# RWKV attention and a relu-squared MLP on one core: w loaded as one row and spread by TensorE, PSUM banks given out by the planner, and the input matmul of units 8 to 19 for two units at a time

## The chip, the core and the metric

The kernel runs on one core of a Trainium2 chip. The metric is the device time of one execution in microseconds (us), as a median of runs. TensorE (PE) multiplies matrices and writes to PSUM; VectorE (DVE), ScalarE (ACT) and GpSimd (POOL) work elementwise; SyncE (SP) only issues transfers here. Each engine runs its own instructions in order and waits on semaphores for the others. Transfers are carried by 16 DMA engines, whichever queue issued them.

## The reference

A linear attention with decay over a sequence of 768, for 4 batches and 8 heads of 48, and behind it an MLP on the 3072 rows of 384 that it gives.

```python
for t in range(S):                                   # S = 768
    cur = einsum('bhd,bhe->bhde', u[None] * kt, vt)
    y[:, :, t] = einsum('bhd,bhde->bhe', rt, state + cur)
    state = w[None, :, :, None] * state + einsum('bhd,bhe->bhde', kt, vt)
x = y.transpose(0, 2, 1, 3).reshape(B * S, H * D)    # 3072 x 384
h = x @ w_in                                         # 384 x 2048
r = maximum(h, 0.0)
out = (r * r) @ w_out                                # 2048 x 384
```

## The kernel before

The sequence is cut into 6 chunks of 128 rows; a chunk of one batch is a unit, so there are 24 units, in the order chunk 0 of batches 0 to 3, chunk 1 of batches 0 to 3, and so on. Per unit:

- Three loads of r, k and v on SP's queue (L219, 192 KB each, in pieces of 192 bytes). VectorE scales r by powers of w and k by negative powers into `rkw` (L242, `wpos` and `wneg`), ScalarE casts v to `vb` (L246).
- `rkw` is turned into `rkT`: for the first NPE = 8 units by eight TensorE transposes into PSUM and one ScalarE copy (L262, L266), for the others by one DMA transpose on SP's queue (L251).
- `at`: eight matmuls of turned k by turned r (L279) into two PSUM banks; VectorE masks them into `am` (L287). `diag` (L293) and `dv` (L301) make the term with u. `s` (L309) and L321/L323/L327/L333 carry the state of the batch from chunk to chunk: add, decay, cast to `stb`. `y` (L341, and L347 with the state), then `yb` (L356).
- `yb` is turned into `xT`: for the first NPY = 6 units on TensorE with a ScalarE copy (L368, L372), for the others by a DMA transpose (L361).
- MLP, in four quarters of 512 hidden columns: the input matmul `m1` (L382, 12 matmuls of 128 columns into one bank `h`), relu on ScalarE (L390), square into `g` on VectorE (L398) for quarters 0 and 2 and on ScalarE (L396) for 1 and 3, and the output matmul `m2` (L405, 4 matmuls of 384 columns). Then the copy `osb` (L412) and the store (L416).

The weights are eight transfers on POOL's queue: four quarters of w_in (I0 to I3, L229) and four of w_out (O0 to O3, L233). In front of each stands a small POOL copy (L225) that reads k of some unit, so that a quarter is not issued before that load has landed. The list `front` in the planner's set-up gives the order of unit loads U and quarters: U0, U1, I0, U2, I1, U3, O0, I2, I3, U4, O1, O2, O3, U5. Each quarter is gated on the unit last named before it.

The set-up: w goes out to all partitions as one 192 KB broadcast (L153), and w and u also as columns by partition in four small scattered loads (L164), all on ScalarE's queue. ScalarE takes the logarithm (L176) and two powers (L178, L180). POOL makes `uwb` from the columns (L199, L202) and `wend`, the decay over a chunk, by a chain of squarings (L204, L206).

The order on each engine comes from a planner (`Plan`): each step has an engine, a cost, a rank, the steps it needs, and the buffers it opens and uses; the planner plays the program through with these costs and a lag after each step, and an engine takes the first step by rank whose needs are done and whose buffers are free. What it finds is issued in that order. PSUM is split into fixed pools: two banks for `at` and `s`, one for `y`, three for `h` (and for the turns), two for `o`.

Of the kernel before, what the change touches and what calls it, by code (L numbers as in the profile page):

```python
# [15 lines left out]
class Plan:  # L16
# [4 lines left out]

    def __init__(self):
        self.steps = []
        self.at = {}
        self.users = {}

# [8 lines left out]
    def run(self, room):  # L35
# [7 lines left out]
        queues = {e: [] for e in todo}  # L43
        order = []
# [7 lines left out]
        def fits(s):  # L52
            names = [x[0] for x in s["new"]]
            for name in set(names):
                ring, m = rings[name], room[name]
                for n in range(len(ring) - m, len(ring) - m + names.count(name)):
                    if n >= 0 and not all(done(x) for x in self.users[ring[n]]):
                        return False
            return True

        while left:
            for e, mine in todo.items():
                if free[e] > t + tiny:
                    continue
                for s in mine:
                    if s["move"] and sum(x[1] for x in queues[e]) > 4.0:
                        continue
                    if all(done(self.at[k]) for k in s["needs"]) and fits(s):
                        mine.remove(s)
                        left -= 1  # L70
                        for x in s["new"]:
                            rings[x[0]].append(x)
# [30 lines left out]
def kernel(  # L103
# [21 lines left out]
    NPE = 8  # L125
    NPY = 6
    NPAD = 4
    SQACT = (1, 3)
# [4 lines left out]
    xpool = ctx.enter_context(tc.tile_pool(name="xpool", bufs=6))  # L133
    gpool = ctx.enter_context(tc.tile_pool(name="gpool", bufs=8))
    mpool = ctx.enter_context(tc.tile_pool(name="mpool", bufs=6))
    ps_at = ctx.enter_context(tc.tile_pool(name="ps_at", bufs=2, space=PSUM))
    ps_y = ctx.enter_context(tc.tile_pool(name="ps_y", bufs=1, space=PSUM))
    ps_h = ctx.enter_context(tc.tile_pool(name="ps_h", bufs=3, space=PSUM))
    ps_o = ctx.enter_context(tc.tile_pool(name="ps_o", bufs=2, space=PSUM))
# [8 lines left out]
    tiles = [{} for _ in units]  # L148

    w_bc = const.tile([128, dm], F32)
    nc.scalar.dma_start(  # L153
        out=w_bc, in_=w.rearrange("h d -> (h d)").unsqueeze(0).to_broadcast([128, dm])
    )
    wcol = const.tile([128, HP], F32)
    ucol = const.tile([128, HP], F32)
    nc.vector.memset(wcol, 1.0)
    nc.vector.memset(ucol, 0.0)
    nc.scalar.preload_act_table_set("natural_log_exp_and_others")  # L160
    with nc.allow_non_contiguous_dma(reason="384 decay values by partition"):
        for x, src in ((wcol, w), (ucol, u)):
            for o in range(2):
                nc.scalar.dma_start(  # L164
                    out=x[o * 64 : o * 64 + D, :],
                    in_=src.rearrange("(p o) d -> o d p", o=2)[o],
                )
# [7 lines left out]
    lnw = const.tile([128, dm], F32)  # L175
    nc.scalar.activation(lnw, w_bc, AF.Ln)  # L176
    wpos = const.tile([128, H, D], F32)
    nc.scalar.activation(wpos.rearrange("p h d -> p (h d)"), lnw, AF.Exp, scale=up)  # L178
    wneg = const.tile([128, H, D], F32)
    nc.scalar.activation(wneg.rearrange("p h d -> p (h d)"), lnw, AF.Exp, scale=down)  # L180
# [18 lines left out]
    nc.gpsimd.tensor_tensor(ucol, ucol, wcol, ALU.mult)  # L199
    for o in range(2):  # L200
        sl = slice(o * 64, o * 64 + 64)
        nc.gpsimd.tensor_copy(uwb.rearrange("p a h -> p (a h)")[sl, o :: H + 2], ucol[sl, :])  # L202
    wend_c = const.tile([128, HP], F32)
    nc.gpsimd.tensor_tensor(wend_c, wcol, wcol, ALU.mult)  # L204
    for _ in range(6):
        nc.gpsimd.tensor_tensor(wend_c, wend_c, wend_c, ALU.mult)  # L206
# [6 lines left out]


# [41 lines left out]
    def turn(i, x):  # L256
        t = tiles[i]
        if x == 0:
            t["tp"] = ps_h.tile([128, 2, HP, C], BF16, name="h")
            t["rkT"] = work.tile([128, 2, HP, C], BF16, name="rkT")  # L260
        for p in range(HP):
            nc.tensor.transpose(t["tp"][:, x, p, :], t["rkw"][:, x, p].rearrange("p o e -> p (o e)"), identb)  # L262

    def evict_rk(i):
        t = tiles[i]
        nc.scalar.copy(t["rkT"], t["tp"])  # L266
# [6 lines left out]
    def at(i):  # L273
        t = tiles[i]
        t["at"] = [ps_at.tile([C, HP, C], F32, name="at") for o in range(2)]
# [7 lines left out]

    def mask(i, o):
# [4 lines left out]
    def diag(i):  # L289
        t = tiles[i]  # L290
        t["y"] = ps_y.tile([C, dm + H], F32, name="y")
# [13 lines left out]
    def state_mm(i):  # L305
        t = tiles[i]
        t["s"] = ps_at.tile([128, HP, 2 * D], F32, name="at")
# [49 lines left out]

    def x_dma(i):
        t = tiles[i]
        t["xT"] = xpool.tile([128, NK, C], BF16, name="xT")  # L360
        nc.sync.dma_start_transpose(out=t["xT"], in_=t["yb"])  # L361

    def x_turn(i):
        t = tiles[i]
        t["tp"] = ps_h.tile([128, NK, C], BF16, name="h")
        t["xT"] = xpool.tile([128, NK, C], BF16, name="xT")
# [7 lines left out]
    def mm1(i, q):  # L374
        t = tiles[i]
        if q == 0:
            t["g"] = gpool.tile([128, NF, C], BF16, name="g")
        t["h", q] = ps_h.tile([128, 4, C], F32, name="h")
        for a in range(4):
            f = q * 4 + a  # L380
            for n in range(NK):
                nc.tensor.matmul(  # L382
                    out=t["h", q][:, a, :], lhsT=w_in_sb[:, n, f * 128 : (f + 1) * 128],
                    rhs=t["xT"][:, n, :], start=(n == 0), stop=(n == NK - 1),
                )

    def relu(i, q):
        t = tiles[i]
        t["gr", q] = mpool.tile([128, 4, C], F32, name="gr")
        nc.scalar.activation(t["gr", q], t["h", q], AF.Relu)  # L390

    def square(i, q):
        t = tiles[i]
        g = t["g"][:, q * 4 : q * 4 + 4, :]
        if q in SQACT:
            nc.scalar.activation(g, t["gr", q], AF.Square)  # L396
        else:
            nc.vector.tensor_tensor(g, t["gr", q], t["gr", q], ALU.mult)  # L398

    def mm2(i, q):  # L400
        t = tiles[i]
        if q == 0:
            t["o"] = ps_o.tile([128, dm], F32, name="o")
        for f in range(q * 4, q * 4 + 4):
            nc.tensor.matmul(  # L405
                out=t["o"], lhsT=t["g"][:, f, :], rhs=w_out_sb[:, f, :],
# [6 lines left out]

    def store(i):
# [5 lines left out]
    plan = Plan()  # L420
    PE, ACT, DVE, POOL, SP = "PE", "ACT", "DVE", "POOL", "SP"
    L1, L2 = 10, 16
# [4 lines left out]
    def add(*a, lag=0.30, **kw):  # L427
        plan.add(*a, lag=lag, **kw)

    def copy(*a, **kw):  # L430
        plan.add(*a, lag=1.20, **kw)

    add("w", ACT, 6.0, None, rank=-1e3)
    copy("begin", SP, 0.74, None, rank=-1e3, move=(0.6, 16))
    front = ['U0', 'U1', 'I0', 'U2', 'I1', 'U3', 'O0', 'I2', 'I3', 'U4', 'O1', 'O2', 'O3', 'U5']
# [11 lines left out]
    for i in range(NU):  # L447
# [3 lines left out]
        rank = place.get(f"U{i}", a - 20)  # L451
# [5 lines left out]
        for x in range(2):  # L457
            add(
                ("scale", i, x), DVE, 0.48, do(scale, i, x), rank=a - 4 + 0.1 * x,
                needs=[("rt", i) if x == 0 else ("kt", i), "w", ("scale", i - 1, x) if i else None],  # L460
# [3 lines left out]
            ("vb", i), ACT, 0.44, do(cast_v, i), rank=a + 0.5, needs=[("vt", i), ("scale", i, 1)],  # L464
# [3 lines left out]
        if i < NPE:  # L468
            add(("turn", i, 0), PE, 0.25, do(turn, i, 0), rank=a, needs=both[:1], new=[("h", i, "rk"), ("rkT", i)], uses=[("rkw", i)])
            add(  # L470
                ("turn", i, 1), PE, 0.25, do(turn, i, 1), rank=a - 0.1, needs=[both[1], ("turn", i, 0)],
                uses=[("h", i, "rk"), ("rkw", i)],
            )
            add(("rkT", i), ACT, 0.95, do(evict_rk, i), rank=a, needs=[("turn", i, 1)], uses=[("h", i, "rk"), ("rkT", i)])
        else:
            copy(("rkT", i), SP, 0.45, do(turn_dma, i), rank=a - 30, needs=both, move=(2.0, 32), new=[("rkT", i)], uses=[("rkw", i)])
        add(("rk", i), DVE, 0.37, do(rk, i), rank=a + 1, needs=[("rkT", i)], new=[("rk", i)], uses=[("rkT", i)])
        add(
            ("at", i), PE, 0.43, do(at, i), rank=a + 1, needs=[("rkT", i)], new=[("at", i, 0), ("at", i, 1)], uses=[("rkT", i)],
        )  # L480
        for o in range(2):
            add(
                ("mask", i, o), DVE, 0.645, do(mask, i, o), rank=a + 1 + 0.1 * o, needs=[("at", i)],
                new=[("am", i, o)], uses=[("at", i, o)],
            )
        add(("diag", i), PE, 0.11, do(diag, i), rank=a + 2, needs=[("rk", i)], new=[("y", i)], uses=[("rk", i)])
        add(("dv", i), DVE, 0.5, do(diag_v, i), rank=a + 2, needs=[("diag", i), ("vb", i)], new=[("dv", i)], uses=[("y", i), ("vb", i)])
        if c < NCH - 1:
            add(
                ("s", i), PE, 0.17, do(state_mm, i), rank=a + 2.1, needs=[("scale", i, 1), ("vb", i), ("at", i)],  # L490
# [3 lines left out]
                ("sadd", i), DVE, 0.6, do(state_add, i), rank=a + 2.2,  # L494
                needs=[("s", i), ("stb", before) if c else None], uses=[("at", i, 2)],
            )
            if c > 0:
                add(("sdec", i), DVE, 0.27, do(state_decay, i), rank=a + 4 + 2, needs=[("sadd", i)])
            add(
                ("stb", i), ACT, 0.6, do(state_cast, i), rank=a + 6 + 2,  # L500
                needs=[("sdec" if c else "sadd", i), ("y", before) if c else None],
            )
        add(
            ("y", i), PE, 0.38 if c else 0.21, do(y_mm, i), rank=a + 3,
# [3 lines left out]
        add(("yb", i), DVE, 0.5, do(evict_y, i), rank=a + 3, needs=[("y", i), ("dv", i)], new=[("yb", i)], uses=[("y", i), ("dv", i)])  # L508
# [62 lines left out]
```

## Time and profile before

| | |
|---|---|
| median of three runs | 181.29 us (181.0 to 181.76) |
| the profiled run | 181.37 us |
| its span, first to last instruction | 179.6 us |
| outside the span | 1.77 us |
| last output matmul ends | 176.24 us |
| first turn of `rkw` on TensorE | 6.19 us |
| first input matmul | 17.16 us |
| DMA: all bytes, mean rate | 28.53 MB, 159 GB/s |
| the unit loads, stores and transposes (queue 1) | 74.5% of 16 engines' span |
| the weights (queue 0) | 10.9% |
| the set-up loads (queue 10) | 0.8% |

The page has a row of busy tenths for each engine in 40 slices of 4.49 us. The chain of waits follows the work that ended last back to the start. In a timeline each line has a start, a length, the engine, the line of the kernel, the operation, output and inputs, and in brackets how long the engine stood idle before it and what released it. Lengths of matmul groups there include the modelled end of the last matmul; the chain has only the time until the next group begins. Issues of DMA transfers that each engine makes are shown with a q behind the engine's name.

The weights' quarters, from their issue to their landing in the profiled run: I0 11.01 to 17.1, I1 13.65 to 20.4, O0 18.69 to 24.1, I2 19.58 to 27.4, I3 20.44 to 29.8, O1 23.13 to 32.5, O2 24.02 to 35.2, O3 24.88 to 37.9. The loads of k: unit 0 lands at 6.7, unit 1 at 10.0, unit 2 at 13.1, unit 3 at 18.1, unit 4 at 22.5, unit 5 at 38.5.

### The profile page before, as it was taken

To read this page: it belongs to the slowest core of one execution; us is meant where nothing else is said; L and a number is where in the kernel's file an instruction comes from. 1 tells how busy PE (TensorE), PEld (TensorE's weight loads), DVE (VectorE), ACT (ScalarE), POOL (GpSimd) and SP (SyncE) were. 2 spreads that over 40 slices of the span, in tenths; PEclk is the share of its full clock that TensorE was granted. 3 is DMA by queue.
4 is the path that set the end of the run, shared out by engine and by line. 5 is a ranking of instruction groups with operands and counts; after the bars stand their busy time and mean duration, and the time that the engine had idled before them with its cause. 6 is when DMAs were issued, how large, how long until landed. Compare 5 with 4: busy or idle time off the path is not lost.

```text
span 179.6 us, 5414 instructions
## 1 busy us (share of the span) xinstructions
PE 164.1 (91%) x2258; PEld 130.3 (73%) x2258; DVE 135.6 (76%) x288; ACT 130.1 (72%) x250; POOL 11.2 (6%) x36
## 2 busy tenths in 40 slices
PE   0257798999999999999999999999999999999992
PEld 0135696887787877788878778787877877787861
DVE  3268859875899999999899699789969957763310
ACT  3636378988889788497787878866885876659751
POOL 2261650000000000000000000000000000000000
PEclk9999999999999999999999999999999999999999
DMA  4999999999998998979799878799869799122002
GB/s 95 184 180 207 212 194 185 185 182 179 188 194 184 154 192 163 192 159 173 171 178 201 157 160 159 138 194 218 162 116 216 144 139 273 59 66 69 17 29 89
DMA packets 107432, 28.53 MB, mean 159 GB/s; under 512 B 100624, under 2 KB 107408, under 8 KB 107408
## 3 DMA queue, kind: packets, MB, share of 16 engines
q1 hardware_dynamic: 102720, 24.85, 74.5%
q0 software_dynamic: 3712, 3.15, 10.9%
q10 hardware_dynamic: 976, 0.20, 0.8%
q8 instruction: 17, 0.28, 0.7%
q14 instruction: 7, 0.06, 0.1%
HBM read 20.65 MB, written 4.72 MB: 141 GB/s over the span
## 4 chain that ended last, share of the span: by engine, by line
PE 86%; DMA 9%; SPq 1%; DVE 1%; issue 0%; ACT 0%; POOL 0%; POOLq 0%
PE h L382 37%; PE o L405 35%; DMA kt<-in_k_dram 6%; PE at L279 4%; DMA w_in_sb<-in_moe_w_in_dram 4%; PE y L341 2%; PE y L347 2%; PE at L309 2%; PE h L262 2%; PE y L293 1%; SPq L219 1%; DVE rkw L242 1%; PE h L368 0%; DVE yb L356 0%; ACT osb L412 0%
## 5 line engine op out<-in xcount | busy, mean ns | idle before, releaser
L382 PE MATMUL h<-xT,w_in_sb 128*128 128x128 bf16 x1152 | 81.6, 223 | 1.3 <-DMA w_in_sb<-in_moe_w_in_dram 1.3
L382 PEld LDWEIGHTS <-w_in_sb 128*128 128x128 bf16 x1152 | 71.9, 100 | 9.4 <-DMA w_in_sb<-in_moe_w_in_dram 1.7
L390 ACT ACTIVATE gr<-h 128x512 f32<-128x512 f32 x96 | 56.8, 596 | 27.0 <-PE h L382 26.3
L405 PE MATMUL o<-w_out_sb,g 128*128 128x384 bf16 x384 | 75.9, 326 | 0.0
L405 PEld LDWEIGHTS <-g 128*128 128x128 bf16 x384 | 33.2, 98 | 14.9
L398 DVE TENSOR_TENSOR g<-gr 128x512 bf16<-128x512 f32 x48 | 32.9, 688 | 12.0 <-ACT gr L390 11.7
L287 DVE TENSOR_TENSOR am<-at,smask 128x512 bf16<-128x512 f32 x48 | 30.9, 684 | 9.6 <-PE at L279 9.5
L396 ACT ACTIVATE g<-gr 128x512 bf16<-128x512 f32 x48 | 30.1, 630 | 1.1
L242 DVE TENSOR_TENSOR rkw<-rt,wpos 128x384 bf16<-128x384 f32 x24 | 13.2, 552 | 4.6 <-ACT wpos L178 2.9
L333 ACT CAST stb<-st 64x192 bf16<-64x192 f32 x40 | 13.9, 347 | 3.1 <-DVE st L321 2.6
L262 PE MATMUL h<-identb,rkw 128*128 128x128 bf16 x64 | 7.8, 264 | 9.0 <-DVE rkw L242 8.8
L412 ACT COPY osb<-o 128x384 f32<-128x384 f32 x24 | 11.5, 479 | 6.2 <-PE o L405 5.8
L246 ACT CAST vb<-vt 128x384 bf16<-128x384 f32 x24 | 12.2, 507 | 3.7 <-DMA vt<-in_v_dram 3.5
L356 DVE TENSOR_TENSOR yb<-y,dv 128x384 bf16<-128x384 f32 x24 | 13.4, 557 | 2.0 <-PE y L347 0.7
L242 DVE TENSOR_TENSOR rkw<-kt,wneg 128x384 bf16<-128x384 f32 x24 | 13.2, 551 | 1.4 <-DMA kt<-in_k_dram 1.4
L301 DVE TENSOR_TENSOR dv<-vb,y 128x384 f32<-128x384 bf16 x24 | 13.1, 545 | 1.4 <-PE y L293 1.4
L323 DVE TENSOR_TENSOR st<-at,st 64x192 f32<-64x192 f32 x32 | 11.3, 354 | 1.8 <-PE at L309 1.6
L262 PEld LDWEIGHTS <-rkw 128*128 128x128 bf16 x64 | 4.9, 115 | 10.7 <-DVE rkw L242 10.3
L271 DVE TENSOR_TENSOR rk<-rkT 128x512 bf16<-128x512 bf16 x24 | 10.0, 418 | 1.9 <-ACT rkT L266 1.9
L279 PE MATMUL at<-rkT 64*128 64x128 bf16 x192 | 10.4, 229 | 0.0
L341 PE MATMUL y<-vb,am 128*128 128x48 bf16 x192 | 8.9, 186 | 0.9 <-DVE dv L301 0.9
L279 PEld LDWEIGHTS <-rkT 64*128 64x128 bf16 x192 | 5.9, 98 | 4.4 <-issue 2.3
(40 smaller groups left out, 82.1 us busy)
## 6 DMA issues: line engine op xcount, KB each, us to landing
rt<-in_r_dram SPq DMA_DIRECT2D x24, 192.0 KB, 4.5
kt<-in_k_dram SPq DMA_DIRECT2D x24, 192.0 KB, 4.4
vt<-in_v_dram SPq DMA_DIRECT2D x24, 192.0 KB, 4.5
out_dram<-osb SPq DMA_DIRECT2D x24, 192.0 KB, 2.7
w_in_sb<-in_moe_w_in_dram POOLq DMA_DIRECT2D x4, 384.0 KB, 7.3
w_out_sb<-in_moe_w_out_dram POOLq DMA_DIRECT2D x4, 384.0 KB, 10.3
xT<-yb SPq DMA_TRANSPOSE x18, 3.2
rkT<-rkw SPq DMA_TRANSPOSE x16, 3.2
```

What stands on the lines that cost most here:

```text
L242: nc.vector.tensor_tensor(t["rkw"][:, x, :, :, :D], pair(src), pair(wx), ALU.mult)
L262: nc.tensor.transpose(t["tp"][:, x, p, :], t["rkw"][:, x, p].rearrange("p o e -> p (o e)"), identb)
L279: nc.tensor.matmul(out=t["at"][o][:, p, :], lhsT=t["rkT"][sl, 1, p, :], rhs=t["rkT"][sl, 0, p, :], start=True, stop=True,)
L287: nc.vector.tensor_tensor(am, t["at"][o], smask.unsqueeze(1).to_broadcast([C, HP, C]), ALU.mult)
L301: nc.vector.tensor_tensor(t["dv"], t["vb"], t["y"][:, dm:].unsqueeze(2).to_broadcast([C, H, D]), ALU.mult)
L333: nc.scalar.copy(stb[b][sl, :, o * D : (o + 1) * D], st32[b][sl])
L356: nc.vector.tensor_tensor(t["yb"], t["y"][:, :dm], t["dv"].rearrange("p h d -> p (h d)"), ALU.add)
L382: nc.tensor.matmul(out=t["h", q][:, a, :], lhsT=w_in_sb[:, n, f * 128 : (f + 1) * 128], rhs=t["xT"][:, n, :], start=(n == 0), stop=(n == N ...
L390: nc.scalar.activation(t["gr", q], t["h", q], AF.Relu)
L396: nc.scalar.activation(g, t["gr", q], AF.Square)
L398: nc.vector.tensor_tensor(g, t["gr", q], t["gr", q], ALU.mult)
L405: nc.tensor.matmul(out=t["o"], lhsT=t["g"][:, f, :], rhs=w_out_sb[:, f, :], start=(f == 0), stop=(f == NF - 1),)
```

## The change

- w is loaded as one row (1.5 KB); its logarithm is taken on one partition and spread to all 128 by one fp32 matmul with a row of ones into a PSUM bank, from which both powers are taken. The columns of w and u are loaded as rows of four partitions on SP's queue behind unit 0's k, turned by two TensorE transposes, and copied by VectorE; POOL works from that copy, behind the issue of I0.
- One tile for each of the eight PSUM banks. The planner now gives a step the bank that has been free longest, with at most 4 for `at`, 2 for `y`, 5 for `h`, 2 for `o`.
- `xT` and `g` become tiles of a whole chunk (four units). The input matmul runs for the units in GROUPS: one at a time for units 0 to 7 and 20 to 23, and two at a time for units 8 to 19, in eight steps of six matmuls of 256 columns. Squares go to ScalarE (A) or VectorE (M) by a pattern over the steps, 5 of 8 on ScalarE.
- NPE is 7, NPY 10, NPAD 6. The ScalarE copy of `rkT` is made in two halves, one behind each four turns.
- The last unit's output matmul, copy and store are made in two halves of 192 columns, the second copy on VectorE.
- `front` is U0, I0, U1, U2, I1, U3, I2, U4, I3, O0, O1, O2, O3, U5. Ranks of loads, state steps and output matmuls, costs and the lag (0.15 for 0.30) are changed.

```diff
-    def run(self, room):
+    def run(self, room, banks, count):
...
+            wanted = [name for name in names if name in banks]
+            if wanted:
+                for n, x in held.items():
+                    if x is not None and all(done(u) for u in self.users[x]):
+                        held[n], since[n] = None, max(u["ready"] for u in self.users[x])
+                if sum(x is None for x in held.values()) < len(wanted):
+                    return False
...
-    NPE = 8
-    NPY = 6
-    NPAD = 4
-    SQACT = (1, 3)
+    NPE = 7
+    NPY = 10
+    NPAD = 6
+    SQUARES = 'AMAMAAAM'
+    GROUPS = (1,) * 8 + (2,) * 6 + (1,) * 4
...
-    nc.scalar.dma_start(
-        out=w_bc, in_=w.rearrange("h d -> (h d)").unsqueeze(0).to_broadcast([128, dm])
-    )
+    nc.scalar.dma_start(out=wrow, in_=w.rearrange("h d -> (h d)").unsqueeze(0))
...
+    def columns():
+        nc.sync.dma_start(out=wu[:, 0, :, :D], in_=w.rearrange("(p o) d -> p o d", o=2))
+        nc.sync.dma_start(out=wu[:, 1, :, :D], in_=u.rearrange("(p o) d -> p o d", o=2))
+
+    def spread_log():
+        spread["log"] = bank("h", "log")[:, :dm]
+        nc.tensor.matmul(out=spread["log"], lhsT=ones, rhs=lnw, start=True, stop=True)
+
+    def power(out, scale):
+        nc.scalar.activation(out.rearrange("p h d -> p (h d)"), spread["log"], AF.Exp, scale=scale)
+
+    def spread_columns():
+        spread["cols"] = bank("h", "cols")[:, : 2 * HP].rearrange("p (x a) -> p x a", x=2)
+        for x in range(2):
+            nc.tensor.transpose(spread["cols"][:, x, :], wu[:, x].rearrange("p o d -> p (o d)"), ident4)
...
-    def evict_rk(i):
+    def evict_rk(i, x=slice(None)):
         t = tiles[i]
-        nc.scalar.copy(t["rkT"], t["tp"])
+        nc.scalar.copy(t["rkT"][:, x], t["tp"][:, x])
...
+    def mm1(i, m, s):
...
+        for a in range(4 // m):
+            f = s * (4 // m) + a
+            for n in range(NK):
+                turned = w_in_sb[:, n, f * 128 : (f + 1) * 128]
+                nc.tensor.matmul(
+                    out=t["h", s][:, a], lhsT=turned, rhs=chunks[c]["xT"][:, n, b : b + m, :],
+                    start=(n == 0), stop=(n == NK - 1),
+                )
...
-    L1, L2 = 10, 16
+    L1, L2 = 10, 18
...
-    def add(*a, lag=0.30, **kw):
+    def add(*a, lag=0.15, **kw):
...
-    front = ['U0', 'U1', 'I0', 'U2', 'I1', 'U3', 'O0', 'I2', 'I3', 'U4', 'O1', 'O2', 'O3', 'U5']
+    front = ['U0', 'I0', 'U1', 'U2', 'I1', 'U3', 'I2', 'U4', 'I3', 'O0', 'O1', 'O2', 'O3', 'U5']
...
-        rank = place.get(f"U{i}", a - 20)
+        rank = place.get(f"U{i}", a - 24)
...
-        ld=6, rkw=NPAD, at=2, y=1, h=3, o=2, g=8, rkT=4, vb=4, rk=4, am=8, dv=4, yb=4, xT=6, gr=6, osb=6,
+        ld=6, rkw=NPAD, g=2, rkT=4, vb=4, rk=4, am=8, dv=4, yb=4, xT=3, gr=8, osb=8,
     )
-    for s in plan.run(room):
+    for s in plan.run(room, dict(at=4, y=2, h=5, o=2), len(banks)):
```

## The prediction

> **What bounds the kernel now.** I read the busy shares and the 40 slices first, then the chain of waits in the middle of the run, then the timeline of the first 30 us, because only there and at the very end TensorE is not full.
>
> ```profile
> PE 164.1 (91%) x2258; PEld 130.3 (73%) x2258; DVE 135.6 (76%) x288; ACT 130.1 (72%) x250; POOL 11.2 (6%) x36
> PE   0257798999999999999999999999999999999992
> DMA  4999999999998998979799878799869799122002
> ```
> ```profile
> 100.20 0.33 PE at L279 x8
> 101.28 0.08 PE y L293 x4
> 102.06 0.17 PE at L309 x4
> 102.23 0.65 PE o L405 x4
> 102.88 0.20 PE y L341 x8
> 103.07 0.17 PE y L347 x4
> 103.25 0.67 PE h L382 x12
> ```
> ```profile
> 8.74 2.21 POOL L206 TENSOR_TENSOR wend_c<-wend_c 128x4 f32<-128x4 f32 x6
> 11.01 0.92 POOL L229 DMA_DIRECT2D w_in_sb<-in_moe_w_in_dram  x1
> 13.65 0.78 POOL L229 DMA_DIRECT2D w_in_sb<-in_moe_w_in_dram  x1 [0.28 <-issue]
> ```
> ```profile
> 20.47 1.46 PE L382 MATMUL h<-xT,w_in_sb 128*128 128x128 bf16 x12 [0.63 <-DMA w_in_sb<-in_moe_w_in_dram]
> ...
> 23.23 1.49 PE L382 MATMUL h<-xT,w_in_sb 128*128 128x128 bf16 x12
> ...
> 28.96 0.83 PE L382 MATMUL h<-xT,w_in_sb 128*128 128x128 bf16 x12
> ...
> 45.15 0.40 PE L279 MATMUL at<-rkT 64*128 64x128 bf16 x8
> ```
>
> In the second fence (the chain at 100 us; start, length, step) every length is the time until TensorE issues its next step: input matmul of a quarter 0.67 (I use 0.668), output matmul of a quarter 0.65 (0.652), `at` 0.33, `diag` 0.10, `s` 0.17, `y` 0.20 plus 0.17 with a state. From the timeline at 40 us, four turns of `rkw` cost 0.22 and an x turn 0.17. Times the counts, that is 64.1 + 62.6 + 8.0 + 2.4 + 3.4 + 8.2 + 3.5 (16 half turns) + 1.0 = 153.2 us of TensorE work. TensorE ends its last output matmul at 176.24, so it loses 23.0 us in all. Adding the same prices along its order up to any step, and taking that from the step's start, gives the loss up to there: `at` of unit 5 starts at 45.15 with 24.2 us of work before it, loss 20.95. After that only 2.05 us are lost in 131, spread evenly, which prices rounded down explain. So the middle is bound by TensorE alone, and what an edit can win lies before 45 us or behind 176.24.
>
> The head loses its time in three ways. The weights come late (third fence): quarter 0 of w_in (I0) is issued at 11.01, after unit 1's k and a POOL chain of 2.21 us, and lands 6.1 us later; I1 lands at 20.47. The DMA row is full from slice 2 on. And twelve matmuls take 1.49 at 23.23 but 0.83 at 28.96: half speed until about 26.4 (a step at 26.48 is the first quick one), though the clock column shows 1.00 there. TensorE is dense from 20.47, so the speed came 5.9 us after that.
>
> **The change part by part.** *w as one row.* Gone: the 192 KB broadcast and four scattered column loads of ScalarE's queue. New: one row, a row of logarithms, one fp32 matmul, two powers read from PSUM. The row lands between 1.8 us after its issue at 0.73 (the last stores) and 3.6 (the broadcast): 2.5 to 4.3, I take 3.4. Ln is 0.52, the powers 0.61 each. The fp32 matmul is in no row; between one 384-column matmul (0.33) and four at half speed (1.3), I take 1.2, nearer the upper since it is cold and fp32. `wpos` then stands at 3.4 + 0.5 + 1.2 + 0.2 + 0.6 = 5.9 (5.54 before), `wneg` at 6.5. Unit 0's k lands at about 6.3 (6.69 before, less the broadcast's share), so this part is worth about 0, bounds -0.8 to +0.5. The two small loads in SP's queue behind k are 16 rows; two transposes on TensorE and a copy on VectorE stand in front of unit 0's second scale, which ends near 7.5 (7.33 before). The POOL chain, now behind I0's issue, ends near 10.3; its reader, the first state add, comes after the masks at about 11.3, so it is covered by 1 us.
>
> *The order of weights.* I0 is now gated on unit 0's k, I1 on unit 2's, I2 on unit 3's, I3 and all of w_out on unit 4's; the POOL chain moves behind I0. Loads that meet no weights land 1.0 apart (unit 2's r at 12.0, k at 13.07). A weight quarter occupies the DMA engines 2.45 (10.9% of the span, by 8). So: I0 issued 6.5, lands 12.6. Unit 2's k: 6.3 + 6 x 1.0 + 2.45 = 14.8; I1 issued 15.0, lands 6.1 to 6.8 later (both rows): 21.4. Unit 3's k 17.8, I2 lands about 24.8. Unit 4's k: 17.8 + 3 + 2 x 2.45 = 25.7; I3 lands 32.3. The four quarters of w_out are issued 0.85 apart and land 2.7 apart, as the last four did before (29.8, 32.5, 35.2, 37.9): 35.0, 37.7, 40.4, 43.1. So I0 comes 4.5 us sooner and the last quarter 5.2 us later.
>
> *What TensorE makes of it.* Unit 0 no longer waits for unit 1's turns: `at` starts near 8.9 (11.15 before), masks, `yb` and x turn follow as before and its first input matmul starts near 14.0 (17.16). From there TensorE is dense, so I expect full speed 5.9 later, at 20. In the new order the work before the first use of I1, I3, and each w_out quarter is 6.2, 15.5, 18.0, 20.6, 23.4 and 25.4. Losses at those gates: 21.4 - 6.2 = 15.2; 32.3 - 15.5 = 16.8; 17.0; 17.1; 17.0; 43.1 - 25.4 = 17.7. The last decides: 17.7 against 20.95, a gain of 3.25. Bounds: gates 2 us earlier or later (unit 4's k between no delay by I2 and waiting for all of it), so 1.25 to 5.25.
>
> *Half copies of the turned tile.* The copy of rkT is split in two halves of 0.5 (1.01 before). The second four turns write the bank that the first half is read from, and in the built program they carry a wait on ScalarE. Where they follow at once (units 2, 3 and 5) TensorE stands 0.4 to 0.7 each, 1.6 in all. I cost it at nothing, since the weights' gates end later; without that cover it is 1.6. The Trainium skill, PSUM — Partial Sum Buffer, Terms, says that TensorE and another engine may not touch one bank at the same time; this speaks against halving a copy in one bank, no row here shows such a collision, and by it the 1.6 could not be planned away.
>
> *Two units at a time.* 48 steps of six 256-column matmuls stand for 48 of twelve. A line through 128 columns (55.7 ns) and 384 (163 ns) gives 109.3, so 0.656 a step: 48 x 0.012 = 0.6 gained, bounds 0 to 0.8. The Trainium skill, TensorE: Matmul & The Clock Gate, Back-to-back issue gap, states 81 ns sustained at 128 columns and 131 at 512; an estimate between them, 98 at 256, would make it 48 x 0.38 = 18 us. The row, 0.67 for twelve, decides: weight loads are already hidden.
>
> *Counts.* Groups of four turns are 14 for 16 and x turns 10 for 6: -0.4 + 0.7 = +0.2. SP's queue so loses four x transposes and gains one of rkT; ScalarE gains four x copies of 0.475 and loses one of 1.01. With the pairs TensorE's work is 152.8, 0.4 less. Banks handed out by the planner, 5 of 8 squares on ScalarE: ScalarE gains about 12 x 0.63 = 7.6 us, VectorE loses 8; hidden behind TensorE, whose middle has no wait to remove. The pairs bunch input matmuls seven in a row, so I put 0.5 on the middle (0 to 9, priced below).
>
> *End.* From 176.24 to 179.6 is 3.36: a copy of 0.48, a store that lands 1.9 after issue, and the close. A copy of 192 columns is 0.35 (the state rows) and the store half as long: 3.0 (2.85 to 3.3).
>
> Sum: 176.24 - 3.25 - 0.4 + 0.5 + 3.0 = 176.1 span. The profiled run took 181.37, 1.77 more than its span: 177.9. The median of runs is 0.08 lower: **177.8**.
>
> **The rivals.** *Weights later still.* Loads that met weights before took up to 17.2 us. If unit 4's k waits for all of I2, every gate moves by 2: 179.8. For it: a full DMA row; against: unit 4's k took 5.7 before, beside two weight quarters.
> *Better.* The gates come 2 us sooner and the pairs cost nothing: 177.8 - 2 - 0.5 = 175.3. For it: five transfers less in front.
> *Half speed stays until 26.4.* TensorE reaches I3's use at 34.4, loss 18.9 instead of 17.7: 179.0. Inside my own case's range.
> *Slower: bursts of the paired matmul.* Seven steps (4.6 us) leave ScalarE 7 x 0.596 + 4 x 0.63 = 6.7 us. Five free banks give 3.3 us of lead and hide it; with two left beside `at`, `y` and `o` it is 1.3, and TensorE stands about 1.2 us in each of six groups: 7.2 - 0.5 more, 184.5. It decides the sign from 0.7 us a group. Against it: ScalarE waits 26.3 us for input matmuls now, so it has room.
>
> **How the numbers follow.** My case has 0.60 (175.8 to 180.3), better 0.12, weights later 0.15, bursts 0.10, the change doing nothing to the time 0.03. About 0.5% is what a measurement can tell from no change: 180.4 to 182.2 counts as same. Faster: 0.60 + 0.12 + most of 0.15 less the edge of my case, 0.80; same 0.09; slower 0.11. Range 175.0 to 181.2: it takes in the better case and most of the late weights, and leaves out the bursts.
>
> **What would show it.** First input matmul at 14, of I1's at 21 to 22, the last w_out quarter landing near 43, full speed by 20 to 22, `at` of unit 5 with a loss near 17, a middle without waits, six matmuls in 0.66. A `rkT`-to-turn wait above 2 us in all, or ScalarE named as releaser of input matmuls in units 8 to 19, would show me wrong.

## The result, and the profile after

The changed kernel takes 184.24 us (median of 4 runs, 182.46 to 184.74) against 181.33 (181.0 to 181.76) for the kernel before in the same session: ratio 1.0151, 95% interval 1.0116 to 1.0186. It is 2.9 us slower; 177.8 was forecast. The ratios in this document leave out the executions that were slowed by a disturbance and the medians do not, so one may differ a little from the quotient of the medians beside it. The profiled run after took 183.86 with a span of 182.1.

The busy shares and slices of the page after (in tenths, 40 slices of 4.55 us):

```profile
PE 167.3 (92%) x1994; PEld 128.0 (70%) x1994; DVE 128.6 (71%) x283; ACT 132.8 (73%) x272; POOL 12.1 (7%) x38
...
PE   3577899999899999999999999999999999999992
...
DMA  4999989999869999789998888899788597120212
```

TensorE begins earlier, as was meant (3577 for 0257), but slice 11, from 45.5 to 50.1 us, is an 8 where before there is a 9, and the nines hide whatever is slow or idle by less than a tenth. To see that, I use the ledger of the prediction again: the loss is the start of a step less the TensorE work before it, at the same prices (the last output matmul ends here at its start plus its price).

| loss of TensorE, us | before | after | forecast |
|---|---|---|---|
| at unit 0's `at` | 10.27 | 8.17 | 8.5 (a start at 8.9 less 0.44 of work) |
| at unit 6's `at` | 21.05 | 20.66 | 17.7 |
| from there to the last output matmul | 1.8 | 5.0 | 2.3 |
| TensorE work in all | 153.25 | 152.93 | 152.8 |
| last output matmul to the end of the span | 3.5 | 3.5 | 3.1 (0.36 less) |

The spans add up: -0.3 of work, -0.4 in the head, +3.2 in the middle, nothing at the end, against 2.5 measured (179.6 to 182.1). So there are two things to explain: why 2 us won at unit 0 are almost gone at unit 6, and why the middle loses three.

First the head. What TensorE waited for between 20 and 49 us, by the view of waits of after (total, times, longest); before, this view has only two waits in the stretch, 0.9 in all:

```profile
PE bank L306 <- ACT rkT L310: 1.6, 3, 0.7
PE bank L323 <- ACT rkT L310: 0.4, 1, 0.4
PE bank L389 <- DVE dv L349: 0.2, 1, 0.2
```

None of the gates of the weights is in it. They landed where the prediction put them (I1 21.5, I3 31.6, the quarters of w_out 35.3, 38.0, 41.1 and 43.4; forecast 21.4, 32.3, 35.0, 37.7, 40.4, 43.1), but TensorE came to them 1.7 to 3.4 us late. The timeline of TensorE in after shows unit 3 on its way (start, length, then in brackets the idle time and its releaser):

```profile
20.58 0.63 PE L306 MATMUL bank<-identb,rkw 128*128 128x128 bf16 x4
21.88 0.59 PE L306 MATMUL bank<-identb,rkw 128*128 128x128 bf16 x4 [0.67 <-ACT rkT L310]
22.26 0.53 PE L389 MATMUL bank<-vb,am 128*128 128x48 bf16 x8
23.14 0.61 PE L323 MATMUL bank<-rkT 64*128 64x128 bf16 x8 [0.36 <-ACT rkT L310]
23.68 1.46 PE L436 MATMUL bank<-xT,w_in_sb 128*128 128x128 bf16 x12
```

and ScalarE's timeline of the same moments:

```profile
21.24 0.59 ACT L310 COPY rkT<-bank 128x512 bf16<-128x512 bf16 x1 [0.26 <-PE bank L306]
21.85 0.63 ACT L451 ACTIVATE g<-gr 128x512 bf16<-128x512 f32 x1
22.50 0.59 ACT L310 COPY rkT<-bank 128x512 bf16<-128x512 bf16 x1
```

The second four turns wait for the first half's copy; then a square of another unit stands between the two halves, and `at` waits for the second. From the start of the first half to the end of the second 1.85 us go by, where the whole copy took 1.01. The same holds for units 2 to 6: in each a relu or a square lies between the halves (1.6 to 2.0 us). And the input matmul at 23.68 still takes 1.46, half speed; full speed came at 25.8, not at 20. From unit 4's `at` (32.4) to unit 6's another 1.75 us are lost at full speed, 0.9 of them by unit 6's second four turns, which wait for the first half's copy.

Second the middle. The chain of waits of after at 124 us (start, length, step), to be set beside the chain of before at 100 us in the prediction:

```profile
124.47 0.38 PE bank L323 x8
124.84 1.05 DVE am L335 x2
125.89 0.14 issue
126.04 0.56 DVE dv L349
126.60 0.04 issue
126.64 0.36 PE bank L389 x8
127.00 0.17 PE bank L395 x4
```

Before, the chain ran on TensorE alone. Here it leaves TensorE at `at` and comes back at `y`: masks, then `dv`, then `y`. `y` does not use `dv`, but `dv` reads the bank into which `y` writes, so the program makes `y` wait until `dv` is done. From 49 us on the waits view of after has one line, and that of before none at all:

```profile
PE bank L389 <- DVE dv L349: 1.4, 7, 0.4
```

1.4 is what a trace with modelled ends of matmuls calls idle. In the ledger there is a gap of 0.11 to 0.58 in front of `y` in ten of the units 6 to 23, 3.1 us in all, which is nearly all of the 3.2 of the middle: an output matmul is listed with 0.81 but makes room for the next step after 0.65. In 11 of these 18 units `y` starts within 0.08 us behind the end of `dv`; before, in none.

### The profile page after: what moved, and what is told of

It reads as the page before. It is cut to its first block, busy times and chain, and to the rows that moved or that the text cites. A ratio compares the mean times of both kernels' runs of the same rounds, so it can differ in the third digit from the quotient of the medians.

```text
span 182.1 us, 4931 instructions
## 1 busy us (share of the span) xinstructions
PE 167.3 (92%) x1994; PEld 128.0 (70%) x1994; DVE 128.6 (71%) x283; ACT 132.8 (73%) x272; POOL 12.1 (7%) x38
## 5 line engine op out<-in xcount | busy, mean ns | idle before, releaser
L436 PE MATMUL bank<-xT,w_in_sb 128*128 128x128 bf16 (+1 forms) x864 | 77.0, 241 | 0.0
L460 PE MATMUL bank<-w_out_sb,g 128*128 128x384 bf16 x368 | 70.9, 326 | 0.0
L444 ACT ACTIVATE gr<-bank 128x512 f32<-128x512 f32 x96 | 55.6, 597 | 20.7 <-PE bank L436 19.2
L460 PEld LDWEIGHTS <-g 128*128 128x128 bf16 x368 | 33.1, 98 | 15.6
L335 DVE TENSOR_TENSOR am<-bank,smask 128x512 bf16<-128x512 f32 x48 | 31.1, 685 | 14.9 <-PE bank L323 14.7
L467 ACT COPY osb<-bank 128x384 f32<-128x384 f32 x23 | 10.8, 475 | 7.8 <-PE bank L460 7.6
L349 DVE TENSOR_TENSOR dv<-vb,bank 128x384 f32<-128x384 bf16 x24 | 13.1, 546 | 2.5 <-PE bank L389 1.3
L404 DVE TENSOR_TENSOR yb<-bank,dv 128x384 bf16<-128x384 f32 x24 | 13.3, 556 | 1.6 <-PE bank L389 0.9
L323 PE MATMUL bank<-rkT 64*128 64x128 bf16 x192 | 10.4, 233 | 2.0 <-ACT rkT L310 2.0
L371 DVE TENSOR_TENSOR st<-bank,st 64x192 f32<-64x192 f32 x32 | 11.2, 352 | 0.2
L389 PE MATMUL bank<-vb,am 128*128 128x48 bf16 x192 | 9.3, 187 | 2.1 <-DVE dv L349 1.6
```

The costliest lines, as they stand in the source:

```text
L323: nc.tensor.matmul(out=t["at"][o][:, p, :], lhsT=t["rkT"][sl, 1, p, :], rhs=t["rkT"][sl, 0, p, :], start=True, stop=True,)
L335: nc.vector.tensor_tensor(am, t["at"][o], smask.unsqueeze(1).to_broadcast([C, HP, C]), ALU.mult)
L349: nc.vector.tensor_tensor(t["dv"], t["vb"], t["y"][:, dm:].unsqueeze(2).to_broadcast([C, H, D]), ALU.mult)
L389: nc.tensor.matmul(out=y[:, 2 * p + o, :], lhsT=t[f"am{o}"][:, p, :], rhs=t["vb"][:, 2 * p + o, :], start=False, stop=c == 0 and o == 1 an ...
L404: nc.vector.tensor_tensor(t["yb"], t["y"][:, :dm], t["dv"].rearrange("p h d -> p (h d)"), ALU.add)
L436: nc.tensor.matmul(out=t["h", s][:, a], lhsT=turned, rhs=chunks[c]["xT"][:, n, b : b + m, :], start=(n == 0), stop=(n == NK - 1),)
```

## The experiments

Each changes the kernel after unless it says otherwise, and each stands beside runs of the kernel before on the same chip (its medians there 181.28 to 181.54). "Mended" below means: with `y` planned behind `dv`.

### y behind dv

```diff
-            needs=[("mask", i, 0), ("mask", i, 1), ("vb", i), ("diag", i), ("stb", before) if c else None],
+            needs=[("mask", i, 0), ("mask", i, 1), ("vb", i), ("diag", i), ("dv", i), ("stb", before) if c else None],
```

The program has this wait anyway; the edit only tells the planner, which then puts other work there.

> The changed kernel, with one need more in the planner: y of a unit also needs dv of that unit, the VectorE step that reads the same PSUM bank. Theory A (order, not pairs): from 49 us on the changed kernel loses about 3 us to y standing behind dv; with the need planned, TensorE gets other work there, the y-behind-dv waits in units 6 to 23 go from about 3 us to under 0.5, and the time falls by 2 to 3 us, to 181.2 to 182.2. Rival (bursts of paired input matmuls): the waits only move to another place and the time stays within 1 us of 184.2.

Measured: 178.98 us (178.35 to 179.77), ratio 0.9866 [0.983, 0.9903]. No wait of `y` for `dv` is left and the loss from unit 6 to the end is 2.0. The gain, 5.3, is 2 us more than was expected; the profiled run also has a better head (18.16 at unit 6). Why is open: the edit also reorders the head, and in that run the clock was open for a while from 15.6 us on.

### The lag, in the kernel after and in the kernel before

```diff
-    def add(*a, lag=0.15, **kw):
+    def add(*a, lag=0.30, **kw):
```

> The changed kernel with the planner's lag after a step at 0.30 us, as before, for 0.15. Theory A (the shorter lag put y straight behind the masks, where dv still holds the bank): about half of dv's time is covered again, 1.5 to 2.5 us of the 3 in the middle come back, 181.8 to 183.0. Rival (y meets dv because VectorE's order or load changed, not by the lag): 183.7 to 184.7, and as many waits of y for dv as in the changed kernel.

Measured: 179.83 (178.75 to 180.89), ratio 0.9914 [0.9881, 0.9947]. The head is unchanged (20.92 at unit 6), the middle is 1.8, as before the change; the waits view has no line from 48 us on. So the lag is what brought the wait: with 0.15 the planner puts `y` directly behind the masks, where `dv` is about to run for 0.55; with 0.30 another step of TensorE usually comes between (in 16 of the units 6 to 23, for 8 of 18 with 0.15).

The opposite edit in the kernel before (0.15 for 0.30):

> The kernel before with the planner's lag at 0.15 us in place of 0.30, nothing else. Theory A (the shorter lag by itself puts y on TensorE while dv still reads y's bank): waits of y for dv of 2 to 3 us in the middle, 183.3 to 184.5. Rival (the shorter lag only does harm together with the banks of the planner, the pairs or the squares on ScalarE): 181.0 to 181.9, no such waits.

Measured: 182.53 (181.45 to 182.8), ratio 1.0042 [1.0022, 1.0063]. Slower by 0.8, between the two: the middle loses 3.1 for 1.8, where the changed kernel loses 5.0. The lag does harm alone, but less than in the changed kernel; what in the rest of the change makes it more was not settled.

### One unit at a time

```diff
-    GROUPS = (1,) * 8 + (2,) * 6 + (1,) * 4
+    GROUPS = (1,) * 24
```

> The changed kernel with GROUPS all ones: no unit is paired, all else as in the change. Theory A: pairs are not what costs; 0.6 us more TensorE work, and the y-behind-dv waits stay: 184 to 185. Rival (bursts of paired input matmuls cost about 0.5 to 1.2 us a group): 3 to 5 us faster, 179.5 to 181.5.

Measured: 183.9 (182.83 to 185.74), ratio 1.0105 [1.0066, 1.0144], not told apart from the changed kernel. The pairs are not the main cause. In the profiled run the middle still loses 4.0, with gaps of 2.0 in front of `y` for 3.1, while TensorE has 0.6 more work; so the pairs may bring about one of the 5.0, against the 0.6 that they save. Nor does the waits view above name ScalarE as releaser of an input matmul in units 8 to 19.

### Two banks for the halves, and fillers against half speed

Two banks, for each half its own (`tp` becomes a pair):

```diff
-            t["tp"] = bank("h", i, "rk").bitcast(BF16).rearrange("p (x a c) -> p x a c", x=2, a=HP)
+        t["tp"][x] = bank("h", i, "rk", x).bitcast(BF16)[:, : HP * C].rearrange("p (a c) -> p a c", a=HP)
```

> The changed kernel, with the two halves of the turned r and k in two PSUM banks instead of one. Theory A: the waits of the second four turns for ScalarE (0.4 to 0.9 us each in units 0 to 6, about 4 us of the head) go; since TensorE stays at half speed in the head for other reasons, part of it is lost to what comes next: 1 to 2 us faster than the changed kernel, 182.2 to 183.2. Rival (the weights' landings set the head): no change, 184 to 184.5.

Measured: 181.94 (181.22 to 182.57), ratio 1.0026 [1.0002, 1.005]. The head is better (18.77), the middle as bad (5.5).

Fillers, matmuls whose result nobody reads, to have TensorE busy from 2 us on:

```diff
+    def warm(n):
+        out = bank("h", "warm", n)[:, :128]
+        for x in range(4):
+            nc.tensor.matmul(out=out, lhsT=identb, rhs=identb, start=True, stop=True, skip_group_check=True)
...
+    for n in range(26):
+        add(("warm", n), PE, 0.44, do(warm, n), rank=1e3 + n, needs=["ready"], new=[("h", "warm", n)], lag=0.0)
```

> The changed kernel with 26 groups of four filler matmuls that the planner puts where TensorE would stand idle, nearly all in the first 25 us; their result is read by nobody. Theory C (half speed costs the head): twelve input matmuls take 0.67 instead of 1.2 from 15 to 20 us on, the loss up to unit 5's at falls from 19.5 to 17.5 or 18, 1.5 to 2 us faster than the changed kernel: 182.2 to 182.8. Rival (speed does not depend on what TensorE did before): full speed still from about 26 us, and the fillers cost up to 1 us: 184.2 to 185.2.

Measured: 181.38 (180.55 to 184.52), ratio 0.9986 [0.9964, 1.0008]. Twelve input matmuls take 0.83 from 15.12 on, and the loss at unit 6 falls to 19.45. Half speed was one of the things that held TensorE behind the gates.

The same in the kernel before (30 groups in its pool for `h`):

> The kernel before with 30 groups of four filler matmuls in TensorE's idle places of the head, nothing else. Theory A (the kernel before loses in its head by half speed, since TensorE is dense from 20.5 us and quick only from 26.4): full speed from about 11 us, 2 to 3 us less, 178.3 to 179.5. Rival (the landing of its weights sets the head, and a quicker TensorE only waits for them): 180.8 to 181.8.

Measured: 181.53 (180.84 to 184.3), ratio 1.0022 [0.9998, 1.0046]. With full speed for good at 21.5, after two spells of 6.8 and 3.4 us, the time is the same. TensorE waits for I0, 2.4 us where 0.7 was the longest such wait:

```profile
PE h L387 <- DMA w_in_sb<-in_moe_w_in_dram: 2.4, 1, 2.4
```

The head of the profiled run did gain 1.3 us (19.75 at unit 6). They are lost again behind it: 0.4 in front of unit 9's `y`, and 0.4 by two filler groups that fell between the last output matmuls. So this run does not show that half speed cost nothing in the kernel before.

### Whole copies

```diff
-            for x in range(2):
-                add(
-                    ("rkT", i) if x else ("rkT", i, 0), ACT, 0.46, do(evict_rk, i, x), rank=a + 0.1 * x - 0.1,
-                    needs=[("turn", i, x), ("rkT", i, 0) if x else None], uses=[("h", i, "rk"), ("rkT", i)],
-                )
+            add(("rkT", i), ACT, 0.95, do(evict_rk, i), rank=a, needs=[("turn", i, 1)], uses=[("h", i, "rk"), ("rkT", i)])
```

First on the mended kernel:

> The changed kernel with y planned behind dv (178.98 measured) and with the turned r and k copied by ScalarE at once, as before, for the seven units that TensorE turns. Theory A (the second four turns stand behind the first half's copy, 1.6 us in all, and nothing is won by it): 177.4 to 178.4. Rival (the halves pay, since at of a unit starts half a copy sooner): 179.3 to 180.5. In between: the one makes good the other.

Measured: 177.75 (177.0 to 179.05), ratio 0.9794 [0.9763, 0.9824], the fastest kernel of the study and 2% faster than before. Then alone, `y` and the lag as changed:

> The changed kernel with the turned r and k copied at once, as before, and nothing else (y and the lag as changed). Theory A (the half copies cost 1.2 us by themselves, wherever y stands): 184.24 - 1.2 = 183.0, between 182.5 and 183.5. Rival (the halves cost only where the head is already quick, since half speed covers them): 184.0 to 184.7.

Measured: 181.67 (179.47 to 182.85), ratio 0.9991 [0.996, 1.0021], 2.6 us less than the changed kernel, twice what was expected. In its profiled run the loss at unit 6 is 17.70, the forecast's number. Between 20 and 49 us its waits view has one line:

```profile
PE bank L436 <- ACT xT L424: 0.3, 1, 0.3
```

and unit 3 goes by without a stop that the view lists. TensorE's timeline, and ScalarE's below it:

```profile
20.83 0.63 PE L306 MATMUL bank<-identb,rkw 128*128 128x128 bf16 x4
21.25 0.53 PE L389 MATMUL bank<-vb,am 128*128 128x48 bf16 x8
21.61 1.46 PE L436 MATMUL bank<-xT,w_in_sb 128*128 128x128 bf16 x12
22.99 0.61 PE L323 MATMUL bank<-rkT 64*128 64x128 bf16 x8
```

```profile
21.50 1.01 ACT L310 COPY rkT<-bank 128x1024 bf16<-128x1024 bf16 x1
```

The copy starts later than the first half did and is done at 22.51, where the second half was done at 23.09; an input matmul covers it. Full speed came at 23.9 in this run, 1.9 us sooner, so part of the gain may be the clock. But of the 3.0 us between the two profiled runs at unit 6, 1.5 arise from unit 4's `at` on, where both run at full speed. The middle still loses 5.0.

### What it is about the halves

If the shared bank is the cost, parting the banks must give what the whole copy gives:

> The changed kernel with y planned behind dv (178.98 measured) and the two halves of the turned r and k in two PSUM banks, each copied by itself. Theory A (the shared bank is what costs): as with whole copies, 177.2 to 178.3, no wait of a turn for the first half's copy. Rival (the halves as such cost, by a later second half or a bank more): 178.6 to 180.2.

Measured: 178.96 (178.83 to 180.76), ratio 0.9892 [0.9852, 0.9932]: nothing over the mended kernel, though parted banks had given 2.3 us where `y` was not mended, in a run whose full speed came at 21.4 for 25.8. The turns no longer wait for a first half, but `at` waits for the second as before: 2.4 us of `PE bank L324 <- ACT rkT L311`, 1.5 with whole copies. In ScalarE's order of this kernel too at least one relu or square lies between the halves of units 2 to 6 (1.6 to 2.8 us from start to end). Telling the planner of the turns' wait:

```diff
-                needs=[both[1], ("turn", i, 0)],
+                needs=[both[1], ("turn", i, 0), ("rkT", i, 0)],
```

> The changed kernel with y planned behind dv (178.98 measured), halves in one bank, and the second four turns planned behind the first half's copy, whose wait the program has anyway. Theory A (the wait costs because the planner does not know of it): other work of TensorE stands there, 177.5 to 178.5. Rival (there is no other work in the head, the wait only shows elsewhere): 178.7 to 179.8.

Measured: 178.76 (178.5 to 178.95), ratio 0.9859 [0.9821, 0.9898], nothing either. So on the mended kernel the wait of the turns is not the price by itself; the halves as such are, and the traces suggest how: two copies of 0.59 for one of 1.01, with other work let in between. At unit 6 the profiled runs with halves lose 18.2 to 18.3, that with whole copies 17.8; this is 0.4 to 0.5 of the 1.0 to 1.2 between the medians, and where the rest lies is open. No kernel was run that keeps the halves side by side on ScalarE, so the last step is read from the traces and not shown by an experiment; nor is it settled how much of the 2.3 us of the two banks in the changed kernel was the bank and how much an earlier full speed.

### The order of the weights, and whether the gates come next

The mended kernel with the order of before:

```diff
-    front = ['U0', 'I0', 'U1', 'U2', 'I1', 'U3', 'I2', 'U4', 'I3', 'O0', 'O1', 'O2', 'O3', 'U5']
+    front = ['U0', 'U1', 'I0', 'U2', 'I1', 'U3', 'O0', 'I2', 'I3', 'U4', 'O1', 'O2', 'O3', 'U5']
```

> The changed kernel with y planned behind dv (178.98 measured) and with the order of unit loads and weight quarters of the kernel before. Theory of the prediction (the weights' gates set the head, the new order is worth 3.25): 181.5 to 182.5. Theory A (the clock and the turns set the head, the gates stand 2 us in front of them): 178.5 to 179.8. The new order may also be worse than the old one, since its last quarter lands 5 us later: 177.5 to 178.4.

Measured: 180.2 (178.11 to 180.34), ratio 0.9899 [0.9864, 0.9934]: worse than the mended kernel by 1.2 in the medians, with overlapping intervals. The new order is worth about 1 by the medians, which the intervals do not tell from nothing, and not 3.25.

Three kernels ask what is next once the head is quick. Mended, two banks and fillers; mended and fillers; mended, whole copies and fillers:

> The changed kernel with all three edits: y planned behind dv, the two halves of turned r and k in two PSUM banks, and 26 groups of four filler matmuls in TensorE's idle places of the head (their result is not read). Theory A (three losses that lie on one path, and behind them the weights' gates, which the prediction put at a loss of 17.7): the head cannot go below 17.7 to 18.2 at unit 6's at, the middle adds about 2, the end 3.4, so 177.8 to 179.0, hardly below the 178.98 with y behind dv alone. Theory B (the gates never decide): the gains of the three single edits add, 184.2 - 5.3 - 2.3 - 2.9 = 173.7, or half of the last two, 176.3; a loss at unit 6 below 17 would say so.

> The changed kernel with y planned behind dv and with the filler matmuls, the halves of the turned tile in one bank as in the changed kernel. Theory A (the weights' gates come next): 178.0 to 179.2, as with y behind dv alone, since that kernel's profile already had full speed from about 22 us and a loss of 18.2 at unit 6. Theory B (clock and turns still set the head): 176.0 to 177.5.

> The changed kernel with y planned behind dv, whole copies (177.75 measured) and the filler matmuls in the head. Theory A (behind the copies the weights' gates come next, which stood at a loss of 19.4 in the run of all three edits): 177.2 to 178.4, no gain. Rival (half speed until 21.6 us still sets the head): 175.5 to 176.8.

Measured: 180.11 (179.56 to 180.69), ratio 0.993 [0.9907, 0.9952]; 178.99 (178.14 to 181.25), ratio 0.987 [0.9833, 0.9908]; 178.91 (177.36 to 181.3), ratio 0.9853 [0.9813, 0.9893]. None beats its kernel without fillers. In the first, TensorE is at unit 5 with a loss of 16.94, and at unit 6 with 19.46; between them lies a line of the waits view that was absent in after:

```profile
PE bank L466 <- DMA w_out_sb<-in_moe_w_out_dram: 2.0, 3, 1.0
```

In the third, TensorE also stands 1.2 us for w_out. So with fillers the gates do hold TensorE. Without fillers, in the profiled run of the mended kernel with whole copies, they do not: TensorE comes to all four quarters of w_out 1.6 to 2.3 us late. The gates themselves also move. The last quarter of w_out landed at 43.8 with whole copies and fillers and at 41.3 without fillers, and between 40.3 and 44.3 in the profiled runs of all kernels with this order of loads, since I3, gated on unit 4's k, is issued anywhere from 22.9 to 26.0. Why that varies is open.

Moving I3 and O0 in front of unit 4's loads, in the mended kernel and in the one with whole copies:

```diff
-    front = ['U0', 'I0', 'U1', 'U2', 'I1', 'U3', 'I2', 'U4', 'I3', 'O0', 'O1', 'O2', 'O3', 'U5']
+    front = ['U0', 'I0', 'U1', 'U2', 'I1', 'U3', 'I2', 'I3', 'O0', 'U4', 'O1', 'O2', 'O3', 'U5']
```

> The changed kernel with y planned behind dv (178.98 measured) and with I3 and O0 gated on unit 3's k, in front of unit 4's loads, the rest as changed. The queue of the weights then has no pause from 17.5 us on; estimate from the rows before (2.7 us a quarter): I3 lands near 27.5, O0 30.2, O3 38.3, for 31.6, 35.3, 43.4. Theory A (the gates of w_out come next behind TensorE's own losses): 0.5 to 1.5 us less, 177.5 to 178.5. Rival (unit 4's loads come later and its turns with them): 179.0 to 180.5.

> The changed kernel with y planned behind dv, whole copies (177.75 measured), and I3 and O0 in front of unit 4's loads. Theory A (the gates of the last quarters hold the head, 5 us sooner now): 176.3 to 177.3. Rival (the gates do not hold it, and unit 4's loads come later): 177.6 to 179.0.

Measured: 179.81 (177.44 to 184.09), ratio 0.9813 [0.9783, 0.9843] from half of its runs; and 182.11 (177.75 to 183.67), for which no ratio can be given. The times stay inconclusive, and both profiled runs are among the longer ones. Their traces suggest the trade: O3 lands near 38, about 3 us sooner than in the same kernels without the move (40.3 and 41.3), and no line names a weight, but unit 4's v and unit 5's r land 5 and 10 us later. In the second kernel TensorE waits, between 20 and 52 us, for scaled r and k, which wait for their loads:

```profile
PE bank L306 <- DVE rkw L286: 3.0, 2, 2.0
```

### Both undone

> The changed kernel with whole copies and the lag at 0.30 us, the two edits that undo the two suspected losses with nothing new in the program. Theory A (they add, 179.83 - 1.2 = 178.6): 178.0 to 179.2. Rival (with the longer lag the planner puts other work where the second four turns wait, so the halves cost nothing there): 179.5 to 180.3.

Measured: 180.31 (179.12 to 186.54), ratio 0.9928 [0.9904, 0.9952]. The two gains do not add with this lag: it is no better than the lag alone. Its profiled run has the good head (18.12 at unit 6), but waits 1.9 us once for a quarter of w_in and loses 3.1 in the middle, with 1.0 of waits for `dv`. Why the lag works worse beside whole copies is open; with whole copies, naming the wait to the planner (177.75) works better than a lag that may cover it.

## Why the prediction was wrong

**The middle** is the larger miss: +0.5 was put there for bunched pairs, +3.2 was measured. The step that failed is "hidden behind TensorE, whose middle has no wait to remove". True of before; but the lag was named among the edits and never costed. It decides how soon behind the masks `y` is placed, and a reader of `y` and `dv` could have seen that both touch one bank while the planner's list of needs for `y` lacks `dv`. The waits view of before shows the same wait twice in the head (0.9 us of `y` for `dv` in all), which was the hint. Undoing the lag alone gave 4.4 us, naming the wait 5.3; in their profiled runs the middle loses 1.8 and 2.0, as before the change.

**The head**: 3.25 forecast, 0.4 measured. Two steps failed. The first is "The last decides: 17.7 against 20.95". The quarters did land as computed, the last at a loss of 18.0. But a gate is only the least that TensorE loses there. For the kernel before the same sum gives 37.9 less 20.7 of work, 17.2, where TensorE lost 20.9: it came to its last gate 3.7 us late, by other delays, and in the changed kernel 1.7 late. The second step is "I cost it at nothing, since the weights' gates end later": cover holds only if TensorE is early enough, and it was not, for two reasons. The halves cost more than 1.6: a half took 0.59, not 0.5, and the copies of one unit were pulled apart on ScalarE. And full speed came at 25.8, not "5.9 later, at 20". Each of the two, mended alone, gave 2.6 to 2.9 us (with the reservation above on the clock). They do not add where the copies are whole and `y` mended (178.91 with fillers for 177.75), since TensorE then meets w_out. The prediction's own sign, "A `rkT`-to-turn wait above 2 us in all", was met: 2.2.

That whole copies alone end at 17.70 is luck. In that run the last quarter landed at 40.8, which is a gate at 15.4, and TensorE came to it 2.2 us late.

The Trainium skill, PSUM — Partial Sum Buffer, Terms, says that two engines may not touch one bank at a time. No run shows a collision; the program keeps them apart by a wait. `y` behind `dv` is such a wait, and was the larger loss. For the halves, where the prediction applied it, the runs are divided: apart in two banks they cost 2.3 us less in the changed kernel and the same in the mended one.

**The end**: -0.36 forecast, 0 measured. VectorE copies the second half (0.36 at 178.87, for 0.48), the store is issued at 179.26 and lands at 180.88, 1.62 later, for 1.86 before. So the copy and the store are shorter by 0.36 together, as forecast, though the store is not "half as long". What failed is the term taken as unchanged, "the close": from the last landing to the end of the span 1.21 us go by, for 0.96 before. Why is open. The remaining 0.1 lies between the last matmul and the store's issue.

**Right**: unit 0 (first input matmul at 14.12, forecast 14.0, though unit 0's k landed at 4.6, not 6.3, and I0 at 11.0, not 12.6), the later landings, and the paired step. Its chain line, six matmuls of 256 columns, reads

```profile
118.86 0.66 PE bank L436 x6
```

and over all 48 the median start to start is 0.655 (0.670 for twelve of 128), as drawn from the rows of before, and far from the 0.38 less a step of the estimate from the sustained figures in the Trainium skill, TensorE: Matmul & The Clock Gate, Back-to-back issue gap.

**The rivals**: the forecast of the slower one, 184.5, lies near the 184.24 measured, but by another mechanism: it wanted ScalarE to hold the pairs, and without pairs the time was the same. Nor does its 1.2 us a group follow from its own terms: 6.7 less 4.6 less 1.3 is 0.8, which gives 182.1. "Half speed stays until 26.4" came nearest: full speed at 25.8, and TensorE at I3's use at 34.96 with a loss of 19.45, for its 34.4 and 18.9. Its 179.0 leaves out unit 6's copies and the middle. The forecast itself, 177.8, is what the kernel does with whole copies and `y` mended, 177.75; but with TensorE behind its gates and no gain at the end, so the agreement is in part luck.

## What to carry to other kernels

Where a planner orders the engines, list for each step what the program really makes it wait for, shared PSUM banks included, and compare it with the planner's list: a wait that is absent there costs as soon as a lag or a rank moves. Splitting a copy costs (two of 0.59 for one of 1.01 here), and more when other work slips in between the halves on the engine that copies. A cost that is "covered by a gate" must be added up to the gate with everything else that is covered by it; here the waits for copies and the half speed together were longer than the cover. And a gate is a lower bound: look first how far behind its gates the engine already runs.

## What was not expected of the hardware

The granted clock opens at very different times. In the profiled runs of the kernels without fillers TensorE was at full speed for good from 17.1 us on in one and from 26.4 in another. In the mended kernel's profiled run the records of the clock open at 15.6, close at 19.0 for 3.4 us, and stay open from 22.4. TensorE's timeline shows it, half speed at 14.09, full at 16.69 (0.38 for four turns that take 0.59 to 0.63 at half speed), half at 19.28, full at 22.42 (eleven in 0.79):

```profile
14.09 1.44 PE L436 MATMUL bank<-xT,w_in_sb 128*128 128x128 bf16 x12
...
16.69 0.38 PE L306 MATMUL bank<-identb,rkw 128*128 128x128 bf16 x4 [0.64 <-ACT rkT L310]
...
19.28 1.44 PE L436 MATMUL bank<-xT,w_in_sb 128*128 128x128 bf16 x12
...
22.42 0.79 PE L436 MATMUL bank<-xT,w_in_sb 128*128 128x128 bf16 x11
```

The clock row of its page shows only the closing (a 6 in slice 5); ahead of the first record it reads full speed, which the matmuls deny. With fillers the clock opened at 9 to 11 us in the four changed kernels that had them. The runs that the ratios take in lie up to 2.6 us apart in one kernel (whole copies alone, 179.47 to 182.08); those of the kernel before lie within 2 in each session.
